# Five first loads in another order: the first weight quarter, the first rows, the early rows and the third rows change places on two queues

## The chip, the cores and the metric

The kernel runs on one core of one Trainium2 chip. A core has TensorE (PE in the profile, its weight loads PEld), VectorE (DVE), ScalarE (ACT), GpSimd (POOL) and SyncE (SP). SyncE, ScalarE and GpSimd can each begin DMAs, on a queue of their own; sixteen DMA engines move the data of all of them. The metric is the time of one execution on the device in microseconds, lower is better.

## The reference, cut to what matters

Two layers follow each other, each made of a part A (segmented attention with a recurrent memory) and a part B (linear attention), both over a layer norm of x (2048 rows of 512 numbers in bfloat16):

```python
def _A_ref(x, mem0, Wq, Wk, Wv, Wo, seg_len):
    for s in range(n_seg):                       # 64 segments of 32 rows
        h = jnp.concatenate([mem, xs], axis=1)   # 8 memory rows and 32 rows of x
        q, k, v = (einsum('btd,dhe->bhte', h, W) for W in (Wq, Wk, Wv))   # 32 heads of 128
        p = softmax(where(mask, q k^T * scale, -1e9))
        o = einsum('bhte,hed->btd', p v, Wo)
        mem = o[:, :M, :]
        outs.append(o[:, M:, :])

x = x + _A_ref(_layernorm(x), A_mem0, A_Wq, A_Wk, A_Wv, A_Wo, A_seg_len)
x = x + _B_ref(_layernorm(x), B_wqkv, B_wo)
x = x + _A_ref(_layernorm(x), A_mem0, A_Wq, A_Wk, A_Wv, A_Wo, A_seg_len)
x = x + _B_ref(_layernorm(x), B_wqkv, B_wo)
```

Each weight of part A has 512 x 4096 numbers, 4 MB. The memory makes the segments a chain: segment s + 1 needs the memory rows that come out of segment s.

## The kernel before, in words

x is cut into 16 tiles of 128 rows, a tile into 4 segments of 32 rows. The weights of part A stay on the chip for the whole run (`Wk_sb`, `Wq_sb`, `Wv_sb`, `Wo_sb`). `Wk`, `Wq` and `Wv` are loaded in four quarters each, 128 of the 512 input rows to a quarter, so one quarter has 128 rows of 8 KB, 1 MB; `Wo` comes in eight pieces of 512 KB. SyncE begins all of these, in the order Wk, Wq, Wv, Wo, in the function `load` (L2063).

The order of all work is written out by hand. Every operation is a node that `add` makes; the table `PLACE` gives each node a time in nanoseconds under a key (layer, step, name), the n-th number of a string for the n-th node made under that key. `schedule` sorts all nodes by that time and `emit` writes for each engine its own nodes in that order. An engine works through its nodes strictly in order, with waits on semaphores where a node needs another engine's result or a landed DMA. The times in the table set the order only; the chip runs each node when its engine gets there and its waits are over. A table entry may end in `a` or `v`, which gives an evacuation of PSUM to ScalarE or VectorE.

What happens before the first segment:

- The loads under the key `setup` (L2056 to L2087): the first rows (tile 0 of x) and the third rows (tile 2) by SyncE, then the weights behind them; by ScalarE the early rows (`xe_sb`: the last 8 rows of each segment of tiles 3 to 6, 128 rows of 1 KB) and the initial memory (8 rows), and behind these a load of the activation table. Each x load is 128 rows of 1 KB. The second rows (tile 1) are begun by GpSimd (L2045).
- `spin` (L2174): groups of twelve matmuls on a tile of ones, whose result nobody reads. Nine groups stand at the start of TensorE's order, six more stand ahead of the second quarter's projections. In the trace they are the matmuls of L2186 and, with the weights kept, L2158 on `one_sb`.
- `prepare` (L2409) for tile 0: `layernorm` (L2201) takes mean and variance on VectorE (L2209, L2210), the inverse root in two steps on ScalarE (L2211, L2213), and the normalized rows on VectorE (L2215); TensorE transposes them (L2226, 16 small matmuls); five copies bring them back to SBUF. `early_rows` (L2235) does the same for the early rows (L2243 to L2257), and `prepare` for tile 2 and then tile 1. VectorE's order is: statistics of tile 0, its normalized rows, statistics of the early rows, statistics of tile 2, the normalized early rows, the normalized rows of tile 2, statistics of tile 1, the copy of tile 2's transposed rows.
- `first_left_blocks` (L2375): the projections of the last 8 rows of each segment of tiles 0 to 6 on Wk and then on Wq (the matmuls of L2310). TensorE runs them quarter by quarter: what needs only the first quarter of Wk comes first, between the transposes of tile 0, of the early rows and of tile 2.

After that the 64 segments follow: projections, attention, output projection (L2594), new memory; part B's work on finished tiles is set in between.

Of the kernel before, what the change touches and what calls it, by code (L numbers as in the profile page):

```python
# [13 lines left out]


PLACE = {
# [1645 lines left out]
class _Prog:  # L1662
# [21 lines left out]
    def add(self, engs, fn, cost, reads=(), writes=(), tiles=(), dsem=None, after=(), lat=0.0, quad=(0, 0), mode=0):  # L1684
        nd = _Node()
        nd.lat = lat
        nd.quad = quad
        nd.mode = mode
        nd.key = self.place + (self.count,)
        self.count += 1  # L1690
        nd.engs = (engs,) if isinstance(engs, str) else tuple(engs)
        nd.cost = cost if isinstance(cost, dict) else {e: cost for e in nd.engs}
        nd.fn = fn
        nd.sync = set(after)
        nd.order = {self.before[e] for e in nd.engs if e in self.before}
        nd.tiles = tuple(tiles)
        nd.dsem = dsem
        nd.rows = nd.chunk = None
        nd.eng = nd.know = None
        nd.sig = False  # L1700
        nd.val = 0
        nd.waits = []
        nd.idx = len(self.nodes)
        if dsem is not None:
            self.dma_tot[dsem] = self.dma_tot.get(dsem, 0) + 16
            nd.dval = self.dma_tot[dsem]
        for key in reads:
            st = self.res.setdefault(key, [None, []])
            if st[0] is not None:
                nd.sync.add(st[0])  # L1710
            st[1].append(nd)
        for key in writes:
            st = self.res.setdefault(key, [None, []])
            if st[0] is not None and st[0] is not nd:
                nd.sync.add(st[0])
            for r in st[1]:
                if r is not nd:
                    nd.sync.add(r)
            st[0] = nd
            st[1] = []  # L1720
        for tl in nd.tiles:

            pe = [o for o in tl.ops if o.engs == ("pe",)]
            if nd.engs == ("pe",):
                if pe:
                    nd.order.add(pe[-1])
                nd.sync.update(tl.ops[tl.ops.index(pe[-1]) + 1:] if pe else [])
            else:
                nd.sync.add(pe[-1])
            tl.ops.append(nd)  # L1730
        self.nodes.append(nd)
        return nd
# [143 lines left out]
def bass_interleave_layers__memory_aug_recurrent_mem_tr__linear_attn_block__prompt_kernel(  # L1876
    nc: bass.Bass,
    A_x: bass.AP,
    A_mem0: bass.AP,
    A_Wq: bass.AP,  # L1880
    A_Wk: bass.AP,
    A_Wv: bass.AP,
    A_Wo: bass.AP,
    A_seg_len: bass.AP,
    B_x: bass.AP,
    B_wqkv: bass.AP,
    B_wo: bass.AP,
    out: bass.AP,
):
    _build_kernel(nc, A_x, A_mem0, A_Wq, A_Wk, A_Wv, A_Wo, A_seg_len, B_wqkv, B_wo, out)  # L1890


def _build_kernel(nc, A_x, A_mem0, A_Wq, A_Wk, A_Wv, A_Wo, A_seg_len, B_wqkv, B_wo, out):
# [4 lines left out]
    M = A_mem0.shape[1]  # L1898
# [18 lines left out]
    def sb(name, shape, dt=BF16):  # L1917
        return E(nc.sbuf_tensor(name, shape, dt))
# [6 lines left out]
    x_sb = sb("x_sb", [128, NX, D])  # L1925
# [32 lines left out]
    EARLY = (3, 4, 5, 6)  # L1958
    ER = 32 * len(EARLY)
# [51 lines left out]
    MEM0 = ("vl", 1, 0)  # L2011
    mem0_sb = vleft[:, 1, 0].rearrange("p g d -> p (g d)")[:, 0:512]
# [5 lines left out]
    xe_sb, hTE = e_sb, eq_sb.rearrange("p (c x) -> p c x", c=4)  # L2018

    banks = [E(nc.psum_tensor("pb%d" % j, [128, 512], F32)) for j in range(8)]  # L2020
    P = _Prog(nc, banks)
    add = P.add
# [13 lines left out]
    x_view = A_x[0].rearrange("(t p) d -> t p d", p=128)  # L2036
# [11 lines left out]
    xr_view = A_x[0].rearrange("(n p) d -> n p d", p=32)  # L2048
# [5 lines left out]
        return (t + shift[0]) % NX  # L2054

    P.at(0, -9, "setup")  # L2056
    rows = [add("sp", lambda a, t=t: a.dma_start(x_sb[:, t, :], x_view[t]), 0.45, writes=[("x", t)], dsem="dx0%d" % t, lat=3.5) for t in (0, 2)]
    rows[1].order.add(rows[0])
    add("act", lambda a: a.dma_start(xe_sb[0:ER, :], xr_view[4 * EARLY[0]:4 * EARLY[-1] + 4, 24:32, :]), 0.45, writes=["e"], dsem="dxe", lat=4.0)
    add("act", lambda a: a.dma_start(mem0_sb[0:M, :], A_mem0[0]), 0.45, writes=[MEM0], dsem="dmem", lat=4.0).order.add(P.nodes[2])  # L2060
    late = []

    def load(o, i, nm, lands, dsem=None):  # L2063
        late.append(add("sp", lambda e: e.dma_start(o, i), 0.45, writes=[nm], dsem=dsem or "d%d" % len(late),
                        lat=lands - 0.45 * (1 + len(late))))
        late[-1].order.update(late[-2:-1] or rows[1:])

    for W, v, nm, t in ((Wk_sb, qk_view[1], "Wk", 14.4), (Wq_sb, qk_view[0], "Wq", 24.4)):
        for c in range(4):
            load(W[:, c, :], v[:, c, :], (nm, 0, c), t - 2.6 * (3 - c))  # L2070
    for c in range(4):
        load(Wv_sb[:, c, :], qk_view[2][:, c, :], ("Wv", 0, c), 35.6 - 2.6 * (3 - c))

    for b in range(2):
        for j in range(4):
            u = 16 * b + 4 * j
            load(Wo_sb[:, u:u + 4, :].rearrange("p f m -> p (f m)"),
                 A_Wo[8 * j + 4 * b:8 * j + 4 * b + 4].rearrange("i (x f) m -> (i x) (f m)", f=4), ("Wo", b, j),
                 38.2 + 5.2 * b + 1.3 * j)
# [4 lines left out]
            writes=[("MB", c) for c in range(4)] + ([("qTl", 2, 0), ("qTl", 2, 1), ("kTl", 2, 0), ("kTl", 2, 1)] if n == 1 else []), dsem="dwoB%d" % n, lat=4.0)  # L2084

    P.before["act"] = add("act", lambda a: a.preload_act_table_set("natural_log_exp_and_others"), 1.3)
    P.before["act"].order.update(P.nodes[2:4])  # L2087


    def pool(fn, writes, reads=()):  # L2090
# [24 lines left out]
    for j in range(4):  # L2115
        q = slice(32 * j, 32 * j + 32)
        d = j % 2
# [16 lines left out]
        writes=["selz"])  # L2134
# [10 lines left out]
    def _m0(t, tl=tl):  # L2145
        for c in range(4):
# [4 lines left out]
         writes=["memT0"])  # L2151
# [959 lines left out]
```

## Time and profile before

| | |
|---|---|
| time, median of 3 runs | 1449.56 us (1449.43, 1449.56, 1451.67) |
| the profiled execution, its own time | 1449.76 us |
| its span, first to last instruction | 1447.8 us |
| TensorE busy | 1429.9 us, 99% of the span |
| VectorE busy | 1238.7 us, 86% |
| ScalarE busy | 909.2 us, 63% |
| DMA engines, mean busy share between 4 and 40 us | near 1.0 |
| what they move there | 370 to 430 GB/s |

How to read it: times inside the profile count from the span's first instruction. A busy TensorE in this table includes the filler matmuls of `spin`. The profile's chain of waits goes back from the last instruction to what released it each time; its parts show what set the end. In the timeline each row has a start, a length, an engine, a line and an operation; what stands in brackets is the engine's idle time just before and what ended it. An SPq, ACTq or POOL row of a DMA tells when it is begun, not when its data moves or lands; the DMA view gives the time from there to the landing of the whole load. q1 is the queue of the DMAs that SyncE begins, q10 that of ScalarE, q0 that of GpSimd. A packet is one row of a load or, with GpSimd, some rows together.

### The profile page before, as it was taken

What the parts mean: (1) busy time and instruction counts of PE and PEld (TensorE: products, weight loads), DVE (VectorE), ACT (ScalarE), POOL (GpSimd) and SP (SyncE); (2) the same over time, 40 slices, a digit from 0 to 9 for tenths busy, and PEclk for the clock granted to TensorE, in tenths of its full rate; (3) what the DMA queues carried; (4) which work ended last, traced back from release to release, by engine and by line L of the source; (5) the groups of instructions that cost most, each with busy time, mean ns of one, the idle gap of its engine ahead of it and who ended that gap; (6) DMA issues with size and microseconds to landing.
All of it is one profiled execution on the core that took longest, in us unless ns stands there. A gap on an engine that the chain in (4) does not pass through costs nothing.

```text
span 1447.8 us, 88480 instructions
## 1 busy us (share of the span) xinstructions
PE 1429.9 (99%) x43649; PEld 773.3 (53%) x37041; DVE 1238.7 (86%) x3930; ACT 909.2 (63%) x2618; POOL 203.7 (14%) x407
## 2 busy tenths in 40 slices
PE   9999999999999999999999999999999999999988
PEld 4455555555555555455455555555555555555554
DVE  5888888889888888988988888888888988898878
ACT  4566666675666566566656666666666666666557
POOL 3111111111111110111201111011011011111110
PEclk9999999999999999999999999999999999999999
DMA  9421101111101001112201111111010011011124
GB/s 384 174 66 40 34 24 51 25 26 26 25 18 26 18 22 25 22 22 58 76 13 25 32 29 29 31 29 33 14 32 23 24 29 29 22 29 22 39 72 130
DMA packets 79247, 66.82 MB, mean 46 GB/s; under 512 B 55480, under 2 KB 70648, under 8 KB 77336
## 3 DMA queue, kind: packets, MB, share of 16 engines
q1 hardware_dynamic: 64872, 42.04, 11.1%
q0 software_dynamic: 13840, 18.98, 4.6%
q8 instruction: 316, 5.18, 1.5%
q14 instruction: 59, 0.48, 0.1%
q10 hardware_dynamic: 160, 0.14, 0.0%
HBM read 31.33 MB, written 14.94 MB: 32 GB/s over the span
## 4 chain that ended last, share of the span: by engine, by line
PE 94%; DVE 4%; DMA 1%; ACT 0%; issue 0%; POOL 0%; POOLq 0%
PE pb L2310 35%; PE pb L2158 24%; PE pb L2594 20%; PE pb L2544 3%; PE pb L2800 2%; PE pb L2502 2%; PE pb L2564 2%; PE pb L2466 2%; PE pb L2170 1%; PE pb L2630 1%; DVE Wq_sb L3038 1%; PE pb L2474 1%; DMA x_sb<-in_A_x_dram 0%; DMA dx_sb<-y_sb 0%; DVE Wq_sb L3050 0%
## 5 line engine op out<-in xcount | busy, mean ns | idle before, releaser
L2027 ACT ACTIVATE arena_sb<-pb 128x512 bf16<-128x512 f32 (+3 forms) x1058 | 511.0, 512 | 235.2 <-PE pb L2158 114.2
L2594 PE MATMUL pb<-Wo_sb,arena_sb 128*32 128x256 bf16 x10368 | 324.1, 274 | 4.5 <-issue 2.0
L2310 PE MATMUL pb<-Wk_sb,arena_sb 128*32 128x512 bf16 x3548 | 311.1, 380 | 1.0 <-DVE arena_sb L2028 0.6
L2594 PEld LDWEIGHTS pb<-Wo_sb,arena_sb 128*32 128x32 bf16 x10368 | 266.5, 97 | 44.3 <-DVE arena_sb L2509 12.1
L2332 DVE STREAM_TRANSPOSE arena_sb<-arena_sb 128x256 f32<-128x256 f32 x640 | 259.1, 426 | 31.1 <-ACT arena_sb L2027 24.7
L2310 PE MATMUL pb<-Wv_sb,arena_sb 128*32 128x512 bf16 x3540 | 281.1, 378 | 0.0
L2045 POOL DMA_DIRECT2D dx_sb<-y_sb x246 | 125.5, 514 | 911.0 <-DVE y_sb L2611 454.7
L2158 PE MATMUL pb<-Wq_sb,arena_sb 128*32 128x512 bf16 x2696 | 249.6, 379 | 0.0
L2310 PEld LDWEIGHTS pb<-Wk_sb,arena_sb 128*32 128x32 bf16 x3548 | 98.0, 96 | 190.5 <-issue 130.6
L2310 PE MATMUL pb<-Wq_sb,arena_sb 128*32 128x512 bf16 x2424 | 199.3, 379 | 0.0
L2517 ACT ACTIVATE arena_sb<-pb,arena_sb 128x128 bf16<-128x128 f32 x480 | 146.7, 370 | 56.5 <-DVE arena_sb L2551 22.2
L2519 DVE TENSOR_TENSOR arena_sb<-pb,arena_sb 128x128 bf16<-128x128 f32 (+2 forms) x417 | 169.2, 406 | 9.1
L2027 ACT ACTIVATE outW_sb<-pb 128x256 f32<-128x256 f32 (+2 forms) x170 | 54.3, 339 | 169.4 <-PE pb L2594 122.2
L2158 PE MATMUL pb<-Wk_sb,arena_sb 128*32 128x512 bf16 x1572 | 155.8, 379 | 0.0
L2158 PE MATMUL pb<-Wv_sb,arena_sb 128*32 128x512 bf16 x1580 | 154.1, 379 | 0.0
L2028 DVE CAST arena_sb<-pb 128x512 bf16<-128x512 f32 (+3 forms) x245 | 124.1, 509 | 32.0 <-PE pb L2158 11.5
L2310 PEld LDWEIGHTS pb<-Wv_sb,arena_sb 128*32 128x32 bf16 x3540 | 88.8, 95 | 77.2 <-issue 44.8
L2310 PEld LDWEIGHTS pb<-Wq_sb,arena_sb 128*32 128x32 bf16 x2424 | 67.7, 97 | 108.6 <-issue 77.6
L2544 PE MATMUL pb<-arena_sb 128*32 128x130 bf16 x3072 | 105.4, 219 | 0.1
L2554 DVE STREAM_TRANSPOSE arena_sb<-arena_sb 128x192 f32<-128x192 f32 x256 | 93.1, 364 | 13.4 <-ACT arena_sb L2517 10.7
L2532 DVE TENSOR_TENSOR arena_sb<-arena_sb,wx_sb 128x1280 bf16<-128x1280 bf16 x128 | 102.3, 799 | 1.7 <-ACT arena_sb L2485 0.7
L2611 DVE TENSOR_TENSOR y_sb<-pb,outW_sb 64x256 bf16<-64x256 f32 x162 | 68.8, 424 | 24.0 <-ACT outW_sb L2027 15.4
(136 smaller groups left out, 1814.4 us busy)
## 6 DMA issues: line engine op xcount, KB each, us to landing
Wk_sb<-in_A_Wk_dram SPq DMA_DIRECT2D x4, 1024.0 KB, 9.8
Wq_sb<-in_A_Wq_dram SPq DMA_DIRECT2D x4, 1024.0 KB, 17.6
Wv_sb<-in_A_Wv_dram SPq DMA_DIRECT2D x4, 1024.0 KB, 26.1
Wo_sb<-in_A_Wo_dram SPq DMA_DIRECT2D x8, 512.0 KB, 22.6
xs_scratch<-x_sb POOLq DMA_DIRECT2D x32, 128.0 KB, 2.1
pq_scratch<-arena_sb POOLq DMA_DIRECT2D x23, 128.0 KB, 2.2
xn_scratch<-arena_sb POOLq DMA_DIRECT2D x20, 128.0 KB, 2.4
lk_scratch<-arena_sb POOLq DMA_DIRECT2D x8, 256.0 KB, 5.4
```

What stands on the lines that cost most here:

```text
L2027: return e.activation(o() if callable(o) else o, i() if callable(i) else i, ACTF.Copy)
L2028: return e.tensor_copy(o() if callable(o) else o, i() if callable(i) else i)
L2045: add(eng, lambda e: e.dma_start(o, i), 0.55 if eng == "pool" else 0.66, reads=reads, writes=writes, dsem="%s%d" % (kind, k), lat=lat + (0 ...
L2158: return pe.add_instruction(mybir.InstMatmult(name=nc.get_next_instruction_name(), engine=mybir.EngineType.PE, ins=[pe.lower_ap(x), pe.low ...
L2310: r = pe.matmul(o, blk[:, c, :], w, start=first, stop=last, tile_position=(0, 32 * j))
L2332: add("dve", lambda v: v.transpose(dst, src(img[:, k, :].bitcast(F32))), 0.445, reads=[("img", k, h) for h in range(2)], writes=[dkey])
L2517: x = e.activation(o[:, u, :], i()[:, u, :], ACTF.Copy, scale=r[:, u:u + 1])
L2519: return e.tensor_tensor(o, i(), r.unsqueeze(2).to_broadcast([128, n, 128]), ALU.mult)
L2532: add("dve", lambda v: v.tensor_tensor(Px.rearrange("p b (n j x) -> p b n j x", n=20, j=4), PQx[:, r2].rearrange("p b (n x) -> p b n x", n ...
L2544: r = pe.matmul(pv.f32()[32 * i:32 * i + 32, 130 * k:130 * k + 130], cols(b, k, i), vimg[:, r2, 4 * b + i, :], start=True, stop=True, skip ...
L2554: add("dve", lambda v, b=b, k0=k0: v.transpose(oTb[:, s1, b, :, :, k0:k0 + 3].rearrange("p h j k q e -> p k (h j) (q e)").bitcast(F32), ox ...
L2594: r = pe.matmul(tl.f32()[32 * j:32 * j + 32, 0:256], oT[:, b, f, n, :, :, e], Wo_sb[:, 16 * b + 4 * n + 2 * f + e, 256 * d:256 * d + 256], ...
```

## The change: what it does

Five DMAs of the first 2 us change their place or their engine.

| load | before | after |
|---|---|---|
| first rows (tile 0 of x, 128 KB) | SyncE, first | ScalarE, first |
| early rows (128 KB) | ScalarE, first | SyncE, second |
| third rows (tile 2 of x, 128 KB) | SyncE, second | SyncE, third |
| first quarter of Wk (1 MB) | SyncE, third | SyncE, first |
| initial memory (8 KB) | ScalarE, second | ScalarE, second |

The second quarter of Wk is SyncE's fourth DMA in both, and all loads behind it keep their order. The order of every computing engine's work is as it was, and so is GpSimd's. The edges in `order` only state the new order for the schedule's own assertion.

Of the table's first entry only the first five numbers differ (the rest of the string is left out here):

```diff
-    (0, -9, "setup"): "843 1291 816 1500 1751
+    (0, -9, "setup"): "815 1700 1296 1500 843
...
-    rows = [add("sp", lambda a, t=t: a.dma_start(x_sb[:, t, :], x_view[t]), 0.45, writes=[("x", t)], dsem="dx0%d" % t, lat=3.5) for t in (0, 2)]
-    rows[1].order.add(rows[0])
-    add("act", lambda a: a.dma_start(xe_sb[0:ER, :], xr_view[4 * EARLY[0]:4 * EARLY[-1] + 4, 24:32, :]), 0.45, writes=["e"], dsem="dxe", lat=4.0)
-    add("act", lambda a: a.dma_start(mem0_sb[0:M, :], A_mem0[0]), 0.45, writes=[MEM0], dsem="dmem", lat=4.0).order.add(P.nodes[2])
+    rows = [add(e, lambda a, t=t: a.dma_start(x_sb[:, t, :], x_view[t]), 0.45, writes=[("x", t)], dsem="dx0%d" % t, lat=3.5)
+            for e, t in (("act", 0), ("sp", 2))]
+    rows.append(add("sp", lambda a: a.dma_start(xe_sb[0:ER, :], xr_view[4 * EARLY[0]:4 * EARLY[-1] + 4, 24:32, :]), 0.45, writes=["e"], dsem="dxe", lat=4.0))
+    rows[1].order.add(rows[2])
+    add("act", lambda a: a.dma_start(mem0_sb[0:M, :], A_mem0[0]), 0.45, writes=[MEM0], dsem="dmem", lat=4.0).order.add(P.nodes[0])
...
-        late[-1].order.update(late[-2:-1] or rows[1:])
+        late[-1].order.update(late[-2:-1])
+        rows[2].order.update(late[:1])
+        late[-1].order.update(rows[1:2] if len(late) > 1 else [])
...
-    P.before["act"].order.update(P.nodes[2:4])
+    P.before["act"].order.update([P.nodes[0], P.nodes[3]])
```

2 rows, old and new, of the table PLACE are left out of this document.

## The prediction

> **What bounds the kernel now.** I read the page's busy times and its chain of waits first, to see which engine sets the end.
>
> ```profile
> span 1447.8 us, 88480 instructions
> ...
> PE 94%; DVE 4%; DMA 1%; ACT 0%; issue 0%; POOL 0%; POOLq 0%
> ```
>
> TensorE is the bound nearly everywhere. The change touches five DMAs of the first 2 us and leaves the order of the computing work as it is, so its effect is decided by when TensorE's dense work begins. That stands in the same chain, cut to the first 60 us (start, length, what):
>
> ```profile
> 2.75 6.59 DMA x_sb<-in_A_x_dram
> 9.36 0.69 DVE st_sb L2209
> ...
> 10.23 0.61 PE pb L2310 x8
> ...
> 12.81 0.65 PE pb L2310 x12
> 13.46 0.22 PE pb L2226 x16
> 13.68 23.96 PE pb L2310 x444
> ...
> 45.61 2.11 PE pb L2594 x64
> ```
>
> From 10.23 us on TensorE goes from piece to piece: six filler groups (10.67 to 12.8), then 444 projection matmuls without a hole, 23.96 us / 444 = 54 ns each. Whatever moves the start at 10.23 moves all that follows, until something else is later. Before 10.23 the chain names the second tile of x (GpSimd's queue), which landed at 2.75 + 6.59 = 9.34. What else stands behind that start is in the timeline of the first 11 us (start, length, engine, line):
>
> ```profile
> 0.81 0.88 SPq L2057 DMA_DIRECT2D x_sb<-in_A_x_dram  x2
> 0.82 0.65 ACTq L2059 DMA_DIRECT2D arena_sb<-in_A_x_dram  x1
> ...
> 1.73 2.41 SPq L2064 DMA_DIRECT2D Wk_sb<-in_A_Wk_dram  x4
> ...
> 3.02 0.69 DVE L2209 BATCH_NORM_STATS2 st_sb<-x_sb 128x6 f32<-128x512 bf16 x1 [3.02 <-DMA x_sb<-in_A_x_dram]
> ...
> 4.53 0.47 DVE L2215 TENSOR_SCALAR arena_sb<-x_sb,st_sb 128x512 bf16<-128x512 bf16 x1 [0.60 <-ACT st_sb L2213]
> ...
> 4.92 0.68 DVE L2243 BATCH_NORM_STATS2 st_sb<-arena_sb 128x6 f32<-128x512 bf16 x1
> ...
> 5.63 0.39 PE L2226 MATMUL pb<-id_sb,arena_sb 128*32 128x128 bf16 x16
> ...
> 6.62 0.39 PE L2158 MATMUL pb<-one_sb 128*32 128x256 bf16 x8
> ...
> 7.89 0.41 PE L2257 MATMUL pb<-id_sb,arena_sb 128*32 128x128 bf16 x16 [0.70 <-DVE arena_sb L2249]
> 8.12 0.61 PE L2310 MATMUL pb<-Wk_sb,arena_sb 128*32 128x512 bf16 x8
> 8.56 0.40 PE L2226 MATMUL pb<-id_sb,arena_sb 128*32 128x128 bf16 x16
> 8.78 0.83 PE L2310 MATMUL pb<-Wk_sb,arena_sb 128*32 128x512 bf16 x12
> 9.36 0.69 DVE L2209 BATCH_NORM_STATS2 st_sb<-x_sb 128x6 f32<-128x512 bf16 x1 [0.97 <-DMA x_sb<-in_A_x_dram]
> 10.23 0.61 PE L2310 MATMUL pb<-Wk_sb,arena_sb 128*32 128x512 bf16 x8 [0.62 <-DVE arena_sb L2028]
> ```
>
> The first rows (tile 0) let VectorE start at 3.02; it normalizes tile 0, then the early rows, then tile 2, strictly in that order, and the rest of the prelude hangs on it. There are two cushions: the transposes at 5.63 came 0.6 us after their input was ready (4.53 + 0.47 = 5.0), because filler stood before them; and VectorE sat idle 0.97 us, TensorE 0.62 us, waiting for the second tile.
>
> **The change part by part.** What a load costs here depends on what stands before it in the sixteen DMA engines. These are the DMA view's landings (first rows, early rows, third rows, first weight quarter) and then, for the stretch 2.25 to 2.75, for 2.75 to 3.25 and for 3.25 to 3.75, the packets of each queue: q1 is SyncE's, q10 ScalarE's.
>
> ```profile
> x_sb<-in_A_x_dram SPq DMA_DIRECT2D x1, 128.0 KB, 2.2
> arena_sb<-in_A_x_dram ACTq DMA_DIRECT2D x1, 128.0 KB, 3.0
> x_sb<-in_A_x_dram SPq DMA_DIRECT2D x1, 128.0 KB, 2.8
> Wk_sb<-in_A_Wk_dram SPq DMA_DIRECT2D x1, 1024.0 KB, 5.9
> ...
> q1 hardware_dynamic: 95, 0.08, 47.6%
> q10 hardware_dynamic: 43, 0.04, 39.7%
> ...
> DMA packets 167, 0.15 MB, mean 309 GB/s; under 512 B 16, under 2 KB 167, under 8 KB 167
> ...
> q10 hardware_dynamic: 102, 0.09, 60.7%
> q1 hardware_dynamic: 65, 0.07, 36.9%
> ...
> DMA packets 108, 0.19 MB, mean 389 GB/s; under 512 B 23, under 2 KB 93, under 8 KB 93
> ```
>
> Both queues began an x load at 0.81 and 0.82, yet the first half microsecond went mostly to q1 (the first rows), the next mostly to q10 (the early rows), and q1's third rows, issued at about 1.3, came mostly after those. The queues take turns by whole loads: a load that is under way on an engine is finished before the other queue gets its turn. Packets of 8 KB, the weight quarter's, are absent until 3.25 (167 of 167 are smaller) and 15 of 108 in the next half microsecond: the quarter runs from about 3.4 to its landing at 1.73 + 5.9 = 7.6, 4.2 us.
>
> *First weight quarter to the front of SyncE's queue.* Its data starts when the first rows' data starts now, about 1.9 (landing 0.81 + 2.2 = 3.0, and 128 KB at some 300 GB/s plus the receipt take about 1.1). It lands near 1.9 + 4.2 = 6.1 instead of 7.6. That alone buys nothing: its first user, the projection at 8.12, came straight behind the early rows' transposes at 7.89.
>
> *First rows to ScalarE's queue.* This is the expensive edit. ScalarE's issue takes 0.65 us against some 0.4 on SyncE (two in 0.88), so SyncE's quarter should be on the engines first, and the first rows wait for its end on each engine. Bounds for their landing: 3.0 to 3.9 if they go first (now: first rows 3.0, early rows from the same ScalarE slot 0.82 + 3.0 = 3.8), and 6.1 + 1.1 = 7.2 if a whole load follows a wholly landed quarter. The receipt is common to both, so I add only the transfer, 128 KB at about 420 GB/s = 0.3 us, less a little because the quarter's slowest engine need not be slow twice: **6.3 us**, 3.3 late. An estimate from those rows.
>
> The Trainium skill, "DMA: Bandwidth & Descriptors" (Rules for kernel authors), says that spreading loads over issuing engines doesn't help bandwidth, since all run on the same 16 engines and interleave. By that page a place on ScalarE's queue is no way past the quarter, which speaks against the change; were the queues independent, the sum would start from 3.8 and come out near zero. The packets by queue bear the page out.
>
> *Early and third rows behind the quarter.* They follow the quarter and the first rows: two more loads of 0.3 to 0.5 us, so about 6.8 and 7.3 (now 3.8 and 4.1). With the first rows at 6.3, VectorE wants them at 4.92 + 3.3 = 8.2 and some 0.6 later: hidden, margin about 1.4 us. If the first rows were not late, this cover is gone and the early rows set the pace, (6.3 to 6.8) - 4.92 = 1.4 to 1.9 late at that step. The initial memory keeps its ScalarE slot and is used behind the fillers at 6.62: hidden. The second tile (GpSimd) no longer queues behind a fresh quarter; it lands no later than 9.3 and VectorE wants it later than that.
>
> *The other weights.* SyncE's fourth load stays the second quarter, with as many bytes before it as now. The engines begin big packets earlier, so the stream may end up to 0.5 us sooner; TensorE would wait for it at one place only:
>
> ```profile
> PEld pb L2594 <- DMA Wo_sb<-in_A_Wo_dram: 0.2, 1, 0.2
> ```
>
> *The sum.* VectorE's start moves 3.02 to 6.3: +3.3. The transposes at 5.63 had 0.6 to give: 4.53 + 3.3 + 0.47 = 8.3, +2.7. Three fillers and their 1 us run behind them as now. On ScalarE and VectorE the early rows' chain, which is in order behind the five copies after those transposes, moves by about 2.8, so the transposes at 7.89 go to 10.7 and the last projection before the hole ends at 9.6 + 2.8 = 12.4. The second tile's statistics run at about 11.2, the copy behind them is done by 12.1, and the matmuls of 10.23 follow at about 12.2 to 12.4: the hole of 0.62 us and VectorE's 0.97 us of idling are used up, **+2.0 us**. The 444 matmuls carry that whole. At the output projection TensorE comes 2 us later, after the last output weights, so the 0.2 us wait goes, of which 0.15 counts: **+1.85 us**. The profiled execution took 1449.76 us (span 1447.8 and 2.0 around it), 0.2 above the median 1449.56; counted on the median, 1449.56 + 1.85 = **1451.4 us**. With the first rows between 5.6 and 7.2 this forecast's own range is 1450.6 to 1452.4.
>
> **The rivals.** I count 0.2% (2.9 us: below 1446.7, above 1452.4) as what a measurement of this kernel tells from no change.
>
> *R1: the TensorE clock drops in the new hole; slower.* Today's fillers run without a break into the transposes; then TensorE would stand idle from 5.6 to 8.3, work 1.2 us, and idle again to about 10.7. The view by stretches shows, near the end of the run, what such a hole can do (length, TensorE busy; the figure before the last two is the granted clock):
>
> ```profile
> 1404.72:1408.13 3.41, 0.84 (x24) 0.56 (x23) 2.00 (x6) 0.38 (x1) 0.51 (x1) 1.00 0.21 48
> 1408.13:1411.55 3.42, 3.22 (x64) 2.47 (x68) 2.75 (x7) 0.00 (x0) 0.00 (x0) 0.50 0.13 42
> ```
>
> A stretch of 3.4 us with 0.84 us of matmuls was followed by one at half clock. In the changed kernel 5.3 to 8.7 would hold some 0.35 + 0.4 = 0.75 us. If the clock then halves for 3.4 us, to about 12.1, the work from 10.7 on takes twice as long: +0.7, and up to +1.7 if the slice lies wholly on dense work. Time: 1451.4 + 0.7 to 1.7 = 1452.1 to 1453.1. It decides from the point where a slice falls almost wholly into the hole; where slices begin against the kernel's start I can't tell from one execution, so I give it a quarter. The Trainium skill, "TensorE: Matmul & The Clock Gate" (Why this matters for your kernels), warns only of idle gaps above some 3 us between bursts; by that the 2.7 us hole keeps the clock, and the time stays 1451.4. The stretch above was broken by 0.84 us of work and lost the clock all the same, so the trace is stricter than the page.
>
> *R2: the first rows go first after all; about level.* For it: the two issues are 10 ns apart, and the rows are small. Against: ScalarE's longer issue, and q10's wait now. Then the early rows are the late ones, 1.4 to 1.9 us at 4.92; less VectorE's 0.97 of idling, TensorE starts 0.4 to 0.9 late, less 0.15: 1449.8 to 1450.3. If the queues mixed packet by packet, eight 8 KB packets (0.3 us each at a sixteenth of 420 GB/s) would stand among the rows' eight: landing about 5.3, and 1450.4.
>
> *R3: faster.* R2's order with a stream that ends up to 0.5 us sooner: the wait at the output weights is all that is open, 0.2 us. To that the half-clock slice quoted above can go, if the late hole falls otherwise on the slices: 64 matmuls took 3.2 us there against 2.1 at 45.61, 1.1 to 1.4 us. Together 1448.0 to 1449.4. More can't be had, since the 444 matmuls and the last weights bind together.
>
> **How the numbers follow.** Forecast 0.5, R1 0.25, R2 0.15, R3 0.1. Above 1452.4 lies half of R1 and the forecast's tail, with later first rows: 0.22. Below 1446.7 nothing that I can price: 0.03 for what I overlooked. Between: 0.75. The range takes the forecast, nearly all of R1, R2 and the upper half of R3: 1448.7 to 1453.2.
>
> **What would show it.** Right: VectorE's first statistics start near 6.3 instead of 3.02, the first quarter lands near 6.1, the first transposes come at about 8.3, no idle of VectorE on the second tile, the 444 matmuls begin near 15.7, and the wait at the output weights is gone. R1: filler or projection matmuls at double length between 8 and 14. R2: first statistics before 4, and VectorE waiting for the early rows. I am wrong if the first rows land by 4, or if the 2 us at the start are not found at 45.

## The result, and the profile after

The changed kernel took 1452.72 us in the median of 15 runs (1450.16 to 1455.20), the kernel before 1449.97 us in 15 runs beside them (1446.85 to 1451.94). The ratio is 1.0020, 95% interval 1.0011 to 1.0028: 1.6 to 4.1 us slower. A second series (the last experiment) gave 1.0020 again, 1.0010 to 1.0030. 1451.4 us was predicted; the 1.85 us of the forecast's sum are a ratio of 1.0013, inside both intervals and near their lower ends. The profiled execution took 1450.16 us (span 1448.2); it was the fastest of the 15.

The timeline of the changed kernel's first 11 us (start, length, engine, line; the code that was at L2090 or later in the kernel before is 3 lines lower down here):

```profile
0.80 0.40 ACTq L2057 DMA_DIRECT2D x_sb<-in_A_x_dram  x1
0.81 0.40 SPq L2065 DMA_DIRECT2D Wk_sb<-in_A_Wk_dram  x1
...
1.27 0.71 SPq L2059 DMA_DIRECT2D arena_sb<-in_A_x_dram  x1
...
5.17 0.39 PE L2161 MATMUL pb<-one_sb 128*32 128x256 bf16 x8
5.66 0.69 DVE L2212 BATCH_NORM_STATS2 st_sb<-x_sb 128x6 f32<-128x512 bf16 x1 [5.66 <-DMA x_sb<-in_A_x_dram]
...
7.63 0.41 PE L2229 MATMUL pb<-id_sb,arena_sb 128*32 128x128 bf16 x16 [2.07 <-DVE arena_sb L2218]
...
8.41 0.66 PE L2161 MATMUL pb<-one_sb 128*32 128x256 bf16 x8
...
9.92 0.62 PE L2260 MATMUL pb<-id_sb,arena_sb 128*32 128x128 bf16 x16
10.32 1.07 PE L2313 MATMUL pb<-Wk_sb,arena_sb 128*32 128x512 bf16 x8
```

VectorE starts at 5.66 instead of 3.02, TensorE waits 2.07 us for tile 0, and then the same filler row that took 0.39 us at 5.17 takes 0.66 at 8.41; eight projection matmuls take 1.07 where they took 0.61 before. TensorE runs at about half speed there. The view by stretches says so too (length, TensorE busy; the granted clock is the figure before the last two):

```profile
4.76:8.18 3.41, 1.34 (x56) 0.48 (x28) 1.89 (x5) 0.58 (x3) 3.07 (x6) 1.00 1.04 400
8.18:11.59 3.41, 3.39 (x76) 1.50 (x56) 2.41 (x9) 2.19 (x10) 2.28 (x10) 0.50 1.01 420
```

The chain of waits (start, length, what) carries both into the dense work:

```profile
0.80 4.83 DMA x_sb<-in_A_x_dram
...
15.69 23.96 PE pb L2313 x444
...
47.61 1.96 PE pb L2597 x61
```

The 444 projection matmuls begin at 15.69 instead of 13.68: **+2.01 us**. The output projection begins at 47.61 instead of 45.61 and takes 1.96 instead of 2.11 us, so 0.15 us come back there. The chain now starts with the first rows and not with the second tile. What the DMA view says of the loads, as time from issue to landing (first quarter and first rows, then early and third rows), and the packets of SyncE's queue q1 and ScalarE's q10 between 3 and 4 us:

```profile
Wk_sb<-in_A_Wk_dram SPq DMA_DIRECT2D x1, 1024.0 KB, 5.6
x_sb<-in_A_x_dram ACTq DMA_DIRECT2D x1, 128.0 KB, 4.8
...
arena_sb<-in_A_x_dram SPq DMA_DIRECT2D x1, 128.0 KB, 5.7
x_sb<-in_A_x_dram SPq DMA_DIRECT2D x1, 128.0 KB, 5.8
...
q1 hardware_dynamic: 48, 0.39, 94.0%
q10 hardware_dynamic: 43, 0.04, 12.6%
```

The first rows land at 5.6, ahead of the quarter at 0.81 + 5.6 = 6.4. In one microsecond there are 48 packets of 8 KB (0.39 MB) and 43 of 1 KB, in the next 48 and 47: over these 2 us the two queues alternate row by row. Early rows (7.0) and third rows (7.8) are there before VectorE wants them, at 7.49 and 8.10.

### The profile page after: what moved, and what is told of

The parts are those of the page before. It is cut to its first block, busy times and chain, and to the rows that moved or that the text cites. A ratio compares the mean times of both kernels' runs of the same rounds, so it can differ in the third digit from the quotient of the medians.

```text
span 1448.2 us, 88480 instructions
## 1 busy us (share of the span) xinstructions
PE 1429.8 (99%) x43649; PEld 774.3 (53%) x37041; DVE 1238.4 (86%) x3930; ACT 909.3 (63%) x2618; POOL 203.9 (14%) x407
## 4 chain that ended last, share of the span: by engine, by line
PE 94%; DVE 4%; ACT 0%; issue 0%; DMA 0%
PE pb L2313 35%; PE pb L2161 24%; PE pb L2597 20%; PE pb L2547 3%; PE pb L2803 2%; PE pb L2505 2%; PE pb L2567 2%; PE pb L2469 2%; PE pb L2633 1%; PE pb L2173 1%; DVE Wq_sb L3041 1%; PE pb L2477 1%; DVE Wq_sb L3053 0%; DMA x_sb<-in_A_x_dram 0%; DVE arena_sb L2789 0%
```

## The experiments

Twelve runs in four sittings; the kernel before ran in each on the same chip (medians 1449.35, 1449.4, 1450.83 and 1451.1 us), so kernels are compared by their ratios to it. Of each kernel's diff the lines that matter are shown; "..." stands for the others, such as the lines that give a load its engine.

**First, the clock alone.** Theory A said: the late rows give half of the 2 us and the half clock the other half. The first try filled TensorE's hole.

```diff
...
+            more = 16 if n == 9 and i == 5 else 0
...
-                for u in range(3):
+                for u in range(3 + more):
```

> The changed kernel with the sixth filler group longer by 16 x 4 matmuls (about 1.7 us at full clock), so that TensorE has work while the first rows are late. Theory A (the late first rows cost about 1.0 us of the 2.0, and the hole that they leave on TensorE costs the other 1.0, through a slice of half clock that falls on the first projections): no half-clock slice between 8 and 12 us, the 444 projection matmuls begin at 14.6 to 14.9 instead of 15.69, and the median comes about 1 us below that of the changed kernel, about 1 us above before. Rival B (the late rows cost all of the 2.0 us, the half clock falls on fillers that nobody waits for): the 444 still begin at 15.5 to 15.8 and the time is that of the changed kernel.

Measured: 1458.24 us, ratio 1.0059 (1.0047 to 1.0071), against both theories. The early half-clock slice was gone, but the first rows landed at 6.3 this time, the fillers ran past the point where the transposes were ready, and the 444 matmuls began at 15.88. From there on its profile lost some 8 us more against that of the kernel before (span 1457.8 against 1447.8 us, 2.2 of it already lost at the 444), little by little to the end. 64 more instructions had done something of their own; that was tested with a run of its own, the last below, and the clock with other means.

**Which of the moved loads costs.** Three kernels made parts of the change on the kernel before. In the first only the quarter goes to the front of SyncE's queue:

```diff
-    (0, -9, "setup"): "843 1291 816 1500 1751
+    (0, -9, "setup"): "1291 1700 816 1500 843
...
```

> The kernel before with one part of the change alone: the first weight quarter ahead of the first rows and the third rows on SyncE; the early rows stay first on ScalarE. Theory A (what is issued beside or behind the quarter's 8 KB packets waits for them): the first rows now stand wholly behind the quarter in one queue and land at 6.5 to 7.0, the early rows, packet by packet with the quarter, at about 5.6; the 444 matmuls begin at 16 to 17 and the time is 2.5 to 3.5 us above before. Rival C (the ScalarE queue is what delays the first rows): they land at about 3 as before, and the time is that of before within 0.5 us.

In the second SyncE begins the early rows, the third rows and then the quarter, and ScalarE the first rows:

```diff
-    (0, -9, "setup"): "843 1291 816 1500 1751
+    (0, -9, "setup"): "815 1291 843 1500 1751
...
```

> The other part alone: the first rows and the early rows change queues (first rows first on ScalarE; SyncE begins early rows, third rows, then the quarter). Theory A: no 8 KB packets stand beside the first rows; they land at 3.0 to 3.6, the 444 matmuls begin at 13.7 to 14.0, and the time is that of before within 0.5 us. Rival C (the ScalarE queue): the first rows land after 4.5, and the 444 begin after 14.5.

In the third the first rows stay first, and the quarter goes ahead of the early and third rows, all on SyncE:

```diff
-    (0, -9, "setup"): "843 1291 816 1500 1751
+    (0, -9, "setup"): "843 2100 1700 1500 1291
...
```

> The first rows first on SyncE again, but the quarter right behind them, then the early and the third rows; ScalarE begins only the initial memory. Theory A (any of the small loads that stands behind the quarter is late and VectorE, in order, waits for it): first rows at about 3.0, early rows at about 7; VectorE waits for these, the transposes of the early rows come near 9.4 instead of 7.89, the 444 begin at 14.4 at full clock, up to 15.4 with a half-clock slice, and the time is 0.5 to 1.5 us above before. Rival D (only the lateness of the first rows matters): 444 from 13.7, time of before.

Ratios: 1.0019 (1.0010 to 1.0027), 1.0000 (0.9991 to 1.0008), 1.0012 (1.0003 to 1.0021). From the timelines of the three, in this order, VectorE's work that waits for a moved load: for the first two its first statistics, for the third the statistics of the early rows (its first ran at 2.98).

```profile
7.00 0.69 DVE L2208 BATCH_NORM_STATS2 st_sb<-x_sb 128x6 f32<-128x512 bf16 x1 [7.00 <-DMA x_sb<-in_A_x_dram]
```

```profile
2.89 0.69 DVE L2208 BATCH_NORM_STATS2 st_sb<-x_sb 128x6 f32<-128x512 bf16 x1 [2.89 <-DMA x_sb<-in_A_x_dram]
```

```profile
7.84 0.69 DVE L2242 BATCH_NORM_STATS2 st_sb<-arena_sb 128x6 f32<-128x512 bf16 x1 [2.87 <-DMA arena_sb<-in_A_x_dram]
```

With the quarter in front, rows are late on whichever queue they stand: 7.0 behind it on SyncE, 5.7 (in the changed kernel) beside it on ScalarE's. The first of the three missed one thing that was expected: its early rows, on ScalarE's queue beside the quarter, landed at 6.5 (0.82 + 5.7) and not at 5.6. The packets of each queue between 3 and 4 us and between 4 and 5 us show that they did not alternate with the quarter's; ScalarE's queue moved nothing in the first of these and 5 rows in the second:

```profile
q1 hardware_dynamic: 50, 0.41, 98.6%
...
q1 hardware_dynamic: 55, 0.42, 102.3%
q10 hardware_dynamic: 5, 0.01, 1.4%
```

Here nearly the whole quarter went first. In the changed kernel ScalarE's load was on the engines first (22 packets of q10 to 1 of q1 between 1.5 and 2 us). With the quarter third, the first rows on ScalarE's queue land at 2.9, and the time is that of before; so ScalarE's queue is not the cause. The third kernel shows that the first rows alone don't save the start: VectorE then waits 2.87 us for the early rows. Its profiled execution lost the clock for two slices in a row (9.37 to 16.19) and came to its 444 matmuls at 18.1, 4.4 us late, where 14.4 to 15.4 was expected; it was the slowest of the twelve timed.

The longer issue on ScalarE, 0.65 us in the kernel before, goes with the load and not with the engine: in the changed kernel's timeline ScalarE issues the first rows in 0.40 us, and SyncE the early rows in 0.71.

**The clock again, with as many instructions as before.** Five groups of filler were made wider:

```diff
-            def mm(pe, tl=tl):
-                x = one_sb[:, 0:128].unsqueeze(1).to_broadcast([128, 2, 128])
+            def mm(pe, tl=tl, wide=4 if n == 9 and i >= 4 else 2):
+                x = one_sb[:, 0:128].unsqueeze(1).to_broadcast([128, wide, 128])
...
```

> The changed kernel with five of its first nine filler groups (the fifth to the ninth) at 512 columns a matmul instead of 256: as many instructions as before, but TensorE stays busy longer in front of the late transposes. The matmuls are filler, whose result nobody reads. Theory A (the dense start is 2 us late, half of it from the late first rows and half from the half-clock slice that TensorE's early hole brings): the half-clock slice between 8 and 12 us is gone, the 444 projection matmuls begin at 14.6 to 15.0 us if the first rows land near 5.6 (15.3 if near 6.3), and the median is about 1 us below the changed kernel's 1452.7. Rival B (the clock adds nothing, the late rows cost the whole 2 us): the 444 begin at 15.5 to 15.8 as in the changed kernel, and the time is the changed kernel's.

Measured: 1451.41 us, ratio 1.0012 (1.0003 to 1.0021); the profile kept its clock. But the first rows landed at 6.6, later than in any other run that has them on ScalarE's queue, and three of the five wide groups stand behind the transposes, where they cost as much at full clock as narrow ones at half clock. The 444 began at 16.0, later than A had said for late rows (15.3). The ratio is lower than the changed kernel's 1.0020, with intervals that overlap. As a test of the clock the run is confounded, by my choice of groups. The next took only groups ahead of the transposes:

```diff
-            def mm(pe, tl=tl):
+            def mm(pe, tl=tl, wide=4 if n == 9 and i in (3, 4, 5) else 2):
...
```

> The changed kernel with only three of its first nine filler groups (the fourth, fifth and sixth, all ahead of tile 0's transposes) at 512 columns a matmul instead of 256, as many instructions as before: TensorE's early hole shrinks, and nothing behind the transposes grows. Theory A (the late rows cost about 1.1 us at the dense work, the half clock the rest): no half-clock piece behind the transposes; from VectorE's first statistics to the first of the 444 projection matmuls 9.0 to 9.3 us instead of the changed kernel's 9.7 (second profile) and 10.0 (first); median 0.5 to 1.2 us below the changed kernel's. Rival B (the half clock adds nothing): 9.7 to 10.0 again, time of the changed kernel.

Its timeline and its chain of waits:

```profile
5.58 0.69 DVE L2212 BATCH_NORM_STATS2 st_sb<-x_sb 128x6 f32<-128x512 bf16 x1 [5.58 <-DMA x_sb<-in_A_x_dram]
...
7.55 0.41 PE L2229 MATMUL pb<-id_sb,arena_sb 128*32 128x128 bf16 x16
...
8.55 0.39 PE L2161 MATMUL pb<-one_sb 128*32 128x256 bf16 x8
...
9.84 0.41 PE L2260 MATMUL pb<-id_sb,arena_sb 128*32 128x128 bf16 x16 [0.71 <-DVE arena_sb L2252]
```

```profile
14.84 23.96 PE pb L2313 x444
```

This is the clean case: rows as late as in the changed kernel (5.58), no wait of TensorE at the transposes, the filler behind them at 0.39, and 14.84 - 5.58 = **9.26 us** from VectorE's start to the 444, as A said. So in this profile the late rows alone cost 14.84 - 13.68 = 1.16 us. The times don't bear the rest out: 1453.13 us, ratio 1.0023 (1.0014 to 1.0032), not below the changed kernel's 1.0020. In the profile its lead over the changed kernel was lost again along the run, among other places here:

```profile
422.75 0.23 PE L2547 MATMUL pb<-arena_sb 128*32 128x130 bf16 x3
...
423.69 0.34 PE L2547 MATMUL pb<-arena_sb 128*32 128x130 bf16 x9 [0.71 <-issue]
```

A group of twelve matmuls is cut after the third by 0.71 us in which TensorE waited for nothing that the profile names ("issue"). Such cuts come in some executions and not in others; where they fall is told with the last experiment. A saving of 0.8 us is below what these series can tell, and whether it holds to the end stays open.

**The changed kernel in other phases.** It was profiled two more times unedited, and then timed again:

> The changed kernel once more, unedited, for a second profile with the clock's slices in another phase. Theory A: the first rows land at 5.4 to 6.0 again; if a half-clock slice lies between 7 and 13 us the 444 matmuls begin at 15.3 to 16.2, without one at 14.5 to 15.0. Rival B: they begin at 15.5 to 15.8 either way.

> The changed kernel, unedited, for a third profile. Theory A: first rows at 5.4 to 6.6 us; from VectorE's first statistics to the first of the 444 matmuls 9.0 to 9.3 us if the matmuls from 8 to 13 us run at full rate, 9.5 to 10.2 if part of them runs at half rate.

> The changed kernel, unedited, timed again, for the size of the whole effect. Theory A (all of it is the late start of the dense work, +1.6 to +2.3 us in three profiles): ratio to before 1.0011 to 1.0016. Rival G (something along the run adds to it, such as more stalls of TensorE on its instruction stream): ratio 1.0018 or more, and a profile with more than before's 3.1 us of TensorE waits that are ended by issue.

From the three chains of waits, in this order:

```profile
15.31 23.96 PE pb L2313 x444
```

```profile
15.94 23.96 PE pb L2313 x428
```

```profile
16.67 23.96 PE pb L2313 x408
```

With the first profile the dense work began 2.01, 1.63, 2.26 and 2.99 us late, though the first rows were always there within 0.15 us (VectorE's start at 5.66, 5.57, 5.68, 5.70). From VectorE's start it took 10.03, 9.74, 10.26 and 10.97 us instead of the 9.26 of the one profile at full clock: the clock cost 0.5 to 1.7 us, 1.0 in the mean. In the last of them the slice lay wholly on dense work:

```profile
6.52:9.94 3.42, 1.57 (x56) 0.66 (x32) 2.36 (x7) 2.04 (x11) 2.64 (x9) 1.00 1.02 408
9.94:13.35 3.41, 3.20 (x56) 1.77 (x60) 2.47 (x9) 1.23 (x4) 2.25 (x11) 0.50 1.01 416
```

The second profile shows no drop, because full speed came late: its fillers still took 0.64 us at 8.16, and full rate began after 10.2. It seems that TensorE's hole lay in the stretch that would have brought it at 7.1 (2.53 of 3.42 us busy). The expectation for "without a slice" (14.5 to 15.0) missed this third way, and the third profile's 10.26 us lie just above the 9.5 to 10.2 that were expected with a slice.

The timed series came to 1453.01 us, 1.0020 (1.0010 to 1.0030), rival G's figure; but G's condition failed. TensorE's waits ended by issue were 2.7 us in that profile, 3.1 in the kernel before. (In the other three profiles of the changed kernel they were between 2.3 and 5.1 us, so one profile of each says little.)

**The hole without late rows.** In the kernel before, six groups were made narrow:

```diff
-            def mm(pe, tl=tl):
-                x = one_sb[:, 0:128].unsqueeze(1).to_broadcast([128, 2, 128])
+            def mm(pe, tl=tl, wide=1 if n == 9 and i >= 3 else 8):
+                x = one_sb[:, 0:32].unsqueeze(1).to_broadcast([128, wide, 32])
...
```

> The kernel before, all rows on time, with the fourth to the ninth filler group at 32 columns a matmul instead of 256, as many instructions as before: this makes a hole in TensorE's early work without any late load. Theory A (such a hole costs the clock, and the clock costs time): VectorE's first statistics stay near 3.0 us, matmuls at half rate between 8 and 12 us, the 444 begin at 14.2 to 15.4 instead of 13.7, median 0.5 to 1.7 us above before. Rival B (the hole is harmless): they begin at 13.5 to 13.8, time of before.

The profile speaks for B: full clock from 5.9 us on, the 444 at 13.29. The times speak for A: 1452.64 us, ratio 1.0018 (1.0007 to 1.0028), and they run from 1447.41 to 1456.68, where the kernel before ran from 1447.84 to 1453.61. The profiled execution was the fastest of the twelve, so it shows the lucky phase; that the others lost the clock is likely, and not shown.

**The late hole.** Two filler groups were put where the kernel before has its half-clock slice near 1408 us:

```diff
...
+    for units in (14, 11):
+        add("pe", spare(units), 0.2, reads=["one"], tiles=[tl], mode=9)
```

> The kernel before with two more groups of filler matmuls (56 and 44 of 256 columns, result unread) in TensorE's late hole near 1404 to 1408 us. If the half-clock slice near 1408 us comes from that hole, no slice of it is left there, the out-projection's 64 matmuls behind the hole take about 2 us instead of 3.5, and the median is 0.7 to 1.3 us below the kernel before. Rival: the filler itself delays the work in the hole, or the instruction stream shifts: the same or slower by 0.5 to 3 us, however the clock goes.

The out-projection behind the hole, in the timeline of the kernel before:

```profile
1408.33 3.48 PE L2594 MATMUL pb<-Wo_sb,arena_sb 128*32 128x256 bf16 x64 [1.43 <-DVE arena_sb L2576]
```

and the filler and the same out-projection in this kernel's:

```profile
1405.52 1.71 PE L3078 MATMUL pb<-one_sb 128*32 128x256 bf16 x56 [2.21 <-issue]
...
1407.70 1.39 PE L3078 MATMUL pb<-one_sb 128*32 128x256 bf16 x44
1408.90 0.30 PE L2596 MATMUL pb<-Wo_sb,arena_sb 128*32 128x256 bf16 x4
1409.53 1.82 PE L2596 MATMUL pb<-Wo_sb,arena_sb 128*32 128x256 bf16 x60 [0.34 <-issue]
```

The clock stayed full in this execution (60 matmuls in 1.82 us, where 64 took 3.48), but they begin later. The hole starts with a wait that issue ends, 1.71 us in the kernel before, and the filler did not fill it: it had to wait itself, 2.21 us, and then pushed the work behind it back. Up to the hole this execution led that of the kernel before by 0.8 us, at the end of the out-projection by 0.5 us. The time did not move: 1449.61 us, ratio 1.0002 (0.9993 to 1.0011). No kernel of the study beat the kernel before.

**64 more instructions.** They were put, as matmuls of 8 columns, where TensorE is idle in the kernel before:

```diff
...
+                for u in range(more):
+                    for j in range(4):
+                        r = again(pe, tl.f32()[32 * j:32 * j + 32, 0:8], one_sb[:, 32 * j:32 * j + 32], one_sb[:, 0:8], True, True, (0, 32 * j), True)
```

> The kernel before with 64 matmuls of 8 columns (result unread) at the end of the ninth filler group, where TensorE is idle anyway: some 0.5 us of work hidden in the hole from 6.9 to 7.9 us. Theory F (64 more instructions at the front shift TensorE's stream against the instruction fetches and cost several us over the run, as in the first experiment): the prelude is unchanged, the 444 matmuls begin at 13.7 to 13.9, and the end is 3 to 9 us later, with new idle of TensorE ended by issue. Rival (the first experiment's loss came from something else): the time of before within 0.5 us.

1456.88 us, ratio 1.0049 (1.0033 to 1.0065): 4.8 to 9.4 us for half a microsecond of hidden work. The 444 began only 0.4 us late (14.07). TensorE's waits that issue ended (line; us in total, times, longest), first in the kernel before and then in this one, its four largest:

```profile
PE pb L2594 <- issue: 2.0, 2, 1.7
...
PE pb L2800 <- issue: 0.7, 1, 0.7
...
PE pb L2170 <- issue: 0.4, 1, 0.4
```

```profile
PE pb L2170 <- issue: 3.3, 2, 3.0
...
PE pb L2633 <- issue: 1.9, 4, 0.6
...
PE pb L2567 <- issue: 1.5, 3, 0.8
PE pb L2803 <- issue: 0.8, 1, 0.8
```

Summed over all such rows, 3.1 us in four waits became 9.1 us in fourteen (10.2 in seventeen in the first experiment; both profiles are of the slowest execution of their series). That explains the first experiment's loss, and theory F stands for the size.

The traces also show where these waits fall. The queue q8 carries instructions; this is its row for the kernel before (packets, MB, share):

```profile
q8 instruction: 316, 5.18, 1.5%
```

These are packets of 16 KB, one for every 256 of the 80900 matmuls and weight loads that the trace has of TensorE. Counted in the order of their start, all 89 waits of TensorE that end in "issue" in the timelines of the fourteen profiles stand at the same place of such a block of 256 (number 193 or 194, counted from 0). With packets and blocks paired in order, each wait ends 1.2 to 1.7 us after the end of its packet; over all blocks of the kernel before the median of that distance is 3.0 us. So TensorE waits there for its instructions: place and time of the waits show it, though no row names the queue as what ended them. The wait in the late hole is one of them: it stands at number 79041 in all fourteen profiles and took 1.4 to 3.0 us. 64 more instructions at the front put other work at the edge of every later block. The late filler, 100 matmuls and 100 weight loads, moved the blocks of the last 42 us only, and its kernel took the time of before.

## Why the prediction came out near, point by point

**The first rows' landing was overpriced.** The step that failed is "the queues take turns by whole loads: a load that is under way on an engine is finished before the other queue gets its turn". The changed kernel's rows show the two queues alternating row by row, 48 packets to 43. The premise "SyncE's quarter should be on the engines first" failed with it: the first rows were issued in 0.40 us and began first. So they did not wait for the whole quarter; they landed at 5.5 to 5.7 in the four profiles of the changed kernel, not at 6.3. The 5.3 that R2 gave for mixing "packet by packet" was nearer. The rows of before on which the wrong reading stood (95 to 43, then 65 to 102) came from loads of equal rows in the first microsecond of traffic, and one such switch doesn't show a rule. Nor do the 48 to 43: with the quarter alone in front, the early rows on ScalarE's queue did wait for nearly the whole quarter (6.5 us), as the prediction's rule says. When two queues alternate and when they don't, these runs leave open. What the Trainium skill, "DMA: Bandwidth & Descriptors" (Rules for kernel authors), says of loads from several issuing engines, that they interleave on the same 16 engines, agrees with the 48 to 43. In the kernel with the quarter alone in front, where one queue moved 50 packets between 3 and 4 us and the other none, it did not show.

**The cushions were right.** Of VectorE's +2.6 the transposes took +2.0 (7.63 against 5.63), as the 0.6 us of cushion said. VectorE no longer waits for the second tile, and the hole of 0.62 us was used up. In the clean case (the three wide groups) the start's +2.6 shrank to +1.9 at the transposes and to +1.16 at the 444. Worked with 5.6 in place of 6.3, the prediction's own sum gives about 1.3.

**The clock was underpriced.** R1, the half clock in the new hole, had a quarter. It came in all four profiles, three times as a slice that dropped and once as a slow start that lasted longer, and cost 0.5 to 1.7 us, about the 0.7 to 1.7 that R1 named. So the +2.0 us of the sum was met at the 444 (+2.01 in the first profile) by luck, through two errors that cancel: 3.3 us of lateness priced where 2.6 came, and no clock loss in the likeliest case where about 1.0 came. The median of 1452.72 us lies in the range of 1448.7 to 1453.2, but at R1's price of 1452.1 to 1453.1 and not at the forecast's, and above 1452.4, to which 0.22 was given; over the kernel before beside it, it is 2.75 us. I left the place of the slices open and so took one chance in four; but the hole was long enough that each of the four places that were seen costs something. The Trainium skill, "TensorE: Matmul & The Clock Gate" (What's actually happening), says that the clock is judged in stretches of 3.413 us that run free of the kernel's start; the boundaries at 4.76, 5.04, 6.52 and 10.49 us in the four profiles of one kernel agree. The same page (Why this matters for your kernels) warns of idle gaps above some 3 us; here a gap of 2.07 us, with work on both sides, lost the clock, so the trace is stricter than the page, as the prediction suspected.

**The rest of the sum.** The 0.15 us at the output weights came back (2.11 to 1.96). Early and third rows were hidden. The quarter landed at 6.4 and not 6.1, which nobody waited for. "ScalarE's longer issue" was a misreading: the issue is the early rows' own, on either engine.

**R2's order fell** (VectorE started at 5.66 and not before 4). **R3's second half showed in the first profile**: the slice at half clock near 1408 was missing there, which gave back about 1.3 us and let that execution end only 0.4 us behind before's. In the last profile two slices fell in that place. The four profiles of the changed kernel have none, none, one and two such slices there, that of the kernel before has one; so it is part of the 5 us by which each kernel's own runs differ.

**What stays open.** Rows (1.16) and clock (1.0 in the mean), less 0.15, make +2.0 us. The medians differ by 2.75 and by 1.9 us in the two series. The interval holds +2.0, but the kernel with the clean start shows no gain in its times, so either the spread hides it or something along the run takes it. The profiles don't settle it. Three of the four of the changed kernel are of executions as fast as its fastest timed one (1450.0 to 1450.2 us); only the last, with a start 2.99 us late, lies at the median. And the late start was carried along but not to the end. This is one step of the chain near the end of the segments, in the kernel before and in the first profile of the changed kernel:

```profile
1380.16 0.30 PE pb L2502 x8
```

```profile
1381.59 0.30 PE pb L2505 x8
```

At that step the four are 1.43, 2.16, 0.84 and 2.27 us behind, at the end of their spans 0.4, 0.3, 0.4 and 3.3. The late hole lies between, with its wait for instructions and its clock.

## What to carry to other kernels

When a load moves ahead of a small one that starts the work, price the small one as late on whichever queue it stands, between two bounds: alternation, row against row, on the shared engines (128 KB of 1 KB rows beside 1 MB of 8 KB rows landed at 5.6 us instead of 3.0), and a wait for the whole large load (6.5 us on the other queue, 7.0 on the same one). Ask of each new hole ahead of dense TensorE work what share of a 3.4 us stretch stays busy, and give the loss of the clock its price in the likeliest case. Before adding filler instructions to a long program, change their width rather than their number, and ask first whether the hole is itself a wait for instructions: more instructions don't fill that.

## What the runs showed of the hardware

- **The clock has two thresholds, not one.** Stretches of 3.41 us with 0.54, 0.84, 1.23, 1.34, 1.57 or 1.58 us of busy TensorE were followed by half clock; those with 1.85 (fifth experiment), 1.93 (the narrow groups) or 2.71 us (before) were not. The lower threshold is not sharp in busy time: in the late hole the second profile of the changed kernel kept its clock with 1.51 us, and the kernel with the quarter alone in front with 1.63. At half clock, 2.50 and 2.53 busy microseconds did not bring full speed back, 2.60 (the changed kernel, 1.35 to 4.76 us), 2.88 and 2.95 did. (Ahead of its first full-speed stretch an execution has no entry in the clock's column; there the length of the fillers tells the rate.)

```profile
6.38:9.79 3.41, 1.85 (x48) 0.40 (x24) 2.58 (x7) 1.27 (x7) 2.74 (x8) 1.00 1.03 422
```

```profile
5.95:9.37 3.42, 1.58 (x64) 0.64 (x28) 1.50 (x4) 0.97 (x6) 2.81 (x9) 1.00 1.05 390
9.37:12.78 3.41, 2.50 (x48) 1.46 (x52) 2.03 (x8) 1.56 (x6) 2.13 (x11) 0.50 1.02 420
12.78:16.19 3.41, 3.41 (x56) 0.94 (x24) 0.81 (x2) 0.30 (x2) 3.01 (x7) 0.50 1.01 423
```

```profile
1406.54:1409.95 3.41, 1.51 (x52) 1.26 (x55) 2.88 (x8) 0.38 (x1) 0.51 (x1) 1.00 0.20 46
1409.95:1413.37 3.42, 3.27 (x92) 2.05 (x84) 3.07 (x8) 0.45 (x2) 0.00 (x0) 1.00 0.15 46
```

The first row is the kernel with five wide groups, whose clock stayed; the next three are the kernel with the first rows ahead of the quarter: 1.58 us lost the clock, and 2.50 at half clock kept it lost for one more stretch. The last two are the second profile of the changed kernel, where 1.51 us did not lose it.

- **64 instructions more near the start, which do next to nothing, cost 4.8 to 9.4 us** over a program of 88480, through TensorE waits that no other engine ends and that all stand at the edge of a block of 256 instructions, 1.2 to 1.7 us behind a 16 KB packet of the instruction queue. Two hundred more, 42 us before the end, cost nothing (1.0002).
- **The same order of loads landed its first rows between 5.5 and 6.6 us** in kernels that differ in filler alone. Between 1.5 and 2 us the changed kernel moved 22 rows of them and one row of the quarter, the two kernels with the latest rows (6.3 and 6.6) none of them and 10 rows of the quarter. What sets that order is open.
